# Value products from whole float32 operands, two heads in the two halves of the array

## The chip, the cores and the metric

One core of one Trainium2 chip runs the program. The metric is device time in microseconds (us) of one launch. Engines are named as in the profile: PE (TensorE matmul), PEld (its weight load), DVE (VectorE), ACT (ScalarE), POOL (GpSimd), SP (the queue that issues the DMAs).

## The reference, cut to what matters

```python
scores = q @ k.T / sqrt(64)                     # 4 batches, 8 heads, 576 positions, 64 features
keep   = scores >= max(scores, axis=-1) - tau   # the others become -1e9
attn   = exp(scores - max) over the kept / (their sum + 1e-9)
x      = (attn @ v), heads side by side         # 2304 x 512
h = x @ moe_w_in;  x = (max(h,0) + alpha*min(h,0)) @ moe_w_out     # 512 -> 2048 -> 512
h = x @ moe2_w_in; out = (h * clip(h+3,0,6)/6) @ moe2_w_out        # 512 -> 2048 -> 512
```

The four weight matrices arrive as float64, all else as float32.

## The kernel before

Everything is multiplied in float32r, the float32 form that the array takes in one pass and with fewer bits. To keep float32's accuracy an operand is split: ACT copies it to float32r (`hi`), and DVE or POOL subtracts that from the operand (`lo`, function `split`, L106). A product is then hi·hi + lo·hi + hi·lo.

Attention runs over 16 pairs of heads (4 of each batch), 9 tiles to a pair: eight tiles of 128 query rows, and one (`None` in `TILES`) with the last 64 rows of both heads. In before the four tiles of the first head come first, then `None`, then those of the second. For each tile i the loop at L608 calls, all with the scheduler's high priority:

- `prep` (L332): loads and splits q, k and v of the next pair and transposes q and k; v is loaded at tile 0 and split at tile 6 (hi and lo side by side make 128 columns, tile `vn`). `prep_t` has one product that uses only 64 rows of the array (L309).
- `do_S` (L349): scores of 576 keys, 4 products of 288 columns (8 for `None`), in one of two PSUM tiles.
- `soft_max`, `soft_thr`, `soft_exp`, `soft_keep`: maximum (DVE L372), threshold (DVE L377), exponential (ACT L382), mask and sum (DVE L389).
- `soft_den`, `soft_rc`: the sum on POOL (L395), reciprocal on DVE (L401), scaling on POOL (L403), and a second copy of the last 64 probabilities on POOL (L404).
- `do_T` (L425): four PE transposes of the float32 probabilities (L429), the hi part out of PSUM on ACT (L433), and the lo part on DVE (L438). For tiles 1, 4 and 7 of the first eight pairs PE (L435) and ACT (L436) make the lo part instead.
- `do_R` (L440): after tiles 1, 4, 6 and 8, the last 64 keys of the two or three tiles since: transposes (L448), hi on ACT (L450), lo on DVE (L451).
- `do_PV` (L453): after the same tiles, 9 float32r products against `vn`, each 256 or 320 columns wide (L465): four a pair, 36 products.
- `do_x` (L469): those products give v-hi and v-lo results in the two halves of the partitions; ACT copies one half out (L479), DVE adds (L484) into `xo`, which goes to the first FFN's input.

The two FFNs (three batches of 512 rows, then the last batch with all leftover rows) are cut into groups of 12 products of 512 columns (`h_group`, `o_group`; lines 204, 234, 240). The groups of batches 0 to 2 are queued, and from tile 39 on the loop takes from that queue after each tile, evenly to the last tile. Weights are decoded from float64 while the FFN of batch 0 runs (L127 to L144: three DVE, two ACT and one POOL instruction a chunk, 64 chunks). The order on each engine is the scheduler's. So there are four stretches: attention alone (to about 135 us of the profile), attention with FFN and decoding (to about 435), attention with FFN (to about 915), FFN alone.

Of the kernel before, what the change touches and what calls it, by code (L numbers as in the profile page):

```python
# [32 lines left out]
def kernel(  # L33
# [31 lines left out]
    PE_LO = (1, 4, 7)  # L65
    PE_LO_END = 2 * PB
    # Chunks to a sum of the output.
# [4 lines left out]
    # Columns of a batch: 128 j + p holds position 4 p + j of the first 512; the other 64  # L72
    # positions of all batches make a block of their own.
# [22 lines left out]
    nidentr = const.tile([P, P], F32R, name="nidentr")  # L96
    nc.vector.tensor_single_scalar(nidentr, ident, -1.0, op=ALU.mult)
# [65 lines left out]
    # The FFNs in their order, each with the chunks of its weights; block None is the last  # L163
    # batch together with the last positions of all.
# [90 lines left out]
    # Queries of the two heads' last positions share a tile: each head's are beside zeros.  # L255
# [5 lines left out]

    pairs = [(b, hp) for b in range(B) for hp in range(NP)]
    TILES = [(0, 0), (0, 1), (0, 2), (0, 3), None, (1, 2), (1, 3), (1, 0), (1, 1)]
# [3 lines left out]
    # A pair of heads: of the first 512 positions, 4 to a partition, a block for each of the 4;  # L267
    # the last 64 of the one head are above those of the other, in block 4 between.
    def prep_load(pi, nm):
        if pi >= len(pairs):  # L270
            return
        b, hp = pairs[pi]
        src = {"q": q, "k": k, "v": v}[nm][b, 2 * hp:2 * hp + 2]
        t = a3.tile([P, 2, NB + 1, D], F32, tag="raw", name="raw")
        nc.sync.dma_start(t[:, :, 0:NB, :].rearrange("p h j d -> p h (j d)"),
                          src[:, 0:SM].rearrange("h (p j) d -> p h (j d)", j=NB))
        if nm == "v":
            for a in range(2):
                nc.sync.dma_start(t[64 * a:64 * a + 64, :, NB, :], src[:, SM:S].rearrange("h r d -> r h d"))
        else:  # L280
            for h in range(2):
                nc.sync.dma_start(t[64 * h:64 * h + 64, 0, NB, :], src[h, SM:S])
        st.setdefault(pi, {})["raw" + nm] = t.rearrange("p h j d -> p (h j) d")

    def prep_split(pi, nm):
        raw = st[pi].pop("raw" + nm)
        n = 2 * NB + 1
        if nm == "v":
            n += 1
            t = a2.tile([P, n, 2, D], F32R, tag="vn", name="vn")  # L290
        elif pi == 0 and nm == "q":
            t = a2.tile([P, 2 * NB + 2, 2, D], F32R, tag="vn", name="natq")
# [39 lines left out]
    def prep(pi, t):  # L332
        if pi >= len(pairs):
            return
        if t == 0:
            prep_split(pi, "k")
            prep_load(pi, "v")
# [7 lines left out]
        if t == 6:  # L345
            prep_split(pi, "v")
            prep_load(pi + 1, "q")

    def do_S(i):  # L349
# [3 lines left out]
        if TILES[t] is None:  # L353
            mms = [(qr[pi % 2][:, h, :], h, a) for h in range(2) for a in range(2)]
        else:
            h, j = TILES[t]
            mms = [(s["q"][:, h * W + j * P:h * W + j * P + P], h, a) for a in range(2)]
        for half in range(2):
            for n, (w, h, a) in enumerate(mms):
                nc.tensor.matmul(ps[:, half, 0:SH], lhsT=w, rhs=s["k"][:, a, h * W + half * SH:h * W + half * SH + SH],  # L360
# [6 lines left out]
    def small(nm, bufs=2):  # L367
        return a2.tile([P, 1], F32, tag=nm, name=nm, bufs=bufs)

    def soft_max(i):  # L370
        nmx = small("nmx")
        nc.vector.tensor_reduce(out=nmx, in_=st[i, "s"][:, :, 0:SH], axis=AX.XY, op=ALU.max, negate=True)  # L372
        st[i, "nmx"] = nmx

    def soft_thr(i):
        thr = small("thr")
        nc.vector.tensor_scalar(out=thr, in0=st[i, "nmx"], scalar1=-1.0, scalar2=ntau_sb, op0=ALU.mult, op1=ALU.add)  # L377
        st[i, "thr"] = thr

    def soft_exp(i):  # L380
        e = a3.tile([P, W], F32, tag="e", name="e", bufs=5)
        nc.scalar.activation(v2(e[:, 0:S]), st[i, "s"][:, :, 0:SH], AF.Exp, bias=st.pop((i, "nmx")), scale=1.0)  # L382
        st[i, "e"] = e

    def soft_keep(i):
        e = st[i, "e"]
        sm = small("sm")
        e = e[:, 0:S]
        nc.vector.scalar_tensor_tensor(out=v2(e), in0=st.pop((i, "s"))[:, :, 0:SH], scalar=st.pop((i, "thr")), in1=v2(e),  # L389
                                       op0=ALU.is_ge, op1=ALU.mult, accum_out=sm)  # L390
        st[i, "sm"] = sm

    def soft_den(i):
        den = small("den")
        nc.gpsimd.tensor_scalar(out=den, in0=st.pop((i, "sm")), scalar1=1.0, scalar2=1e-9, op0=ALU.mult, op1=ALU.add)  # L395
        st[i, "d"] = den

    # The last 64 probabilities of a row twice.
    def soft_rc(i):
        rc = small("rc", 3)  # L400
        nc.vector.reciprocal(rc, st.pop((i, "d")))  # L401
        e = st[i, "e"]
        nc.gpsimd.tensor_scalar(out=e[:, 0:S], in0=e[:, 0:S], scalar1=rc, scalar2=0.0, op0=ALU.mult, op1=ALU.add)  # L403
        nc.gpsimd.tensor_scalar(out=e[:, S:W], in0=e[:, SM:S], scalar1=1.0, scalar2=0.0, op0=ALU.mult, op1=ALU.add)  # L404
# [3 lines left out]
    PLACE = [  # L408
        ("u", 0, None), ("u", P, (0, 0, 256)),
        ("w", 0, None), ("w", P, None), ("w", 256, (0, 0, 320)),  # L410
        ("w", 64, None), ("w", 192, (1, 64, 320)),
        ("u", 0, None), ("u", P, (1, 0, 256)),
    ]
    ptb = {}

    def pt_buf(i):
        nm = PLACE[i % NT][0]
        if i % NT in (0, 2, 7):
            ptb[nm] = a1.tile([P, 2 * NB + 1, {"u": 256, "w": 384}[nm]], F32R, tag="pt" + nm, name="pt" + nm,
                              bufs=2 if nm == "u" else 1)  # L420
        return ptb[nm]
# [3 lines left out]
    def do_T(i):  # L425
        e = st[i, "e"]
        ps = ps_t.tile([P, NB, P], F32, tag="t", name="t")
        for j in range(NB):
            nc.tensor.matmul(ps[:, j], lhsT=e[:, P * j:P * j + P], rhs=ident, is_transpose=True, start=(j == 0), stop=True,  # L429
                             skip_group_check=True)  # L430
        nm, c0, _ = PLACE[i % NT]
        pt = pt_buf(i)[:, :, c0:c0 + P]
        nc.scalar.copy(pt[:, 0:NB], ps)  # L433
        if i < PE_LO_END and i % NT in PE_LO:
            nc.tensor.matmul(ps, lhsT=nidentr, rhs=pt[:, 0:NB], start=False, stop=True, skip_group_check=True)  # L435
            nc.scalar.copy(pt[:, NB + 1:], ps)  # L436
        else:
            nc.vector.tensor_tensor(out=pt[:, NB + 1:], in0=ps, in1=f32(pt[:, 0:NB]), op=ALU.subtract)  # L438

    def do_R(i):  # L440
        nm, c0, unit = PLACE[i % NT]
        if unit is None:
            return
        m = [2, 3, 2, 2][[1, 4, 6, 8].index(i % NT)]
        ps = ps_t.tile([P, SM], F32, tag="t", name="r")[:, 0:m * P]
        for j in range(m):
            e = st.pop((i - m + 1 + j, "e"))
# [278 lines left out]
```

## Time and profile before

| | |
|---|---|
| median of 3 runs | 1220.63 us (1220.61 to 1224.99) |
| span of the profiled execution | 1219.0 us |
| PE busy | 1124.4 us, 92%, 6008 instructions |
| DVE busy | 814.9 us, 67% |
| ACT busy | 699.7 us, 57% |
| POOL busy | 770.5 us, 63% |
| DMA | 139.51 MB, 38.9% of 16 engines' span |

The median lies 1.6 us over the span of the profiled execution. The page's shares are averages over stretches that have different limits, so the stretches are read one by one. The starts of matmuls are recorded, their ends are modelled: a product's price in a row of products is the distance between starts, not its own duration.

### The profile page before, as it was taken

The numbers are of one execution on the slowest core, as the hardware profiler recorded it, in microseconds if no ns is written. First come the engines' busy times: TensorE is split into PE (matmuls) and PEld (weight loads), VectorE is DVE, ScalarE is ACT, GpSimd is POOL, SyncE is SP. The second block draws the span as 40 slices with busy tenths as digits, with TensorE's granted clock in tenths as the row PEclk, the third lists the DMA queues.
The fourth block names the chain that finished last, engine by engine and source line by source line (L and its number), as shares of the span: only waits on it lengthen the run. The fifth ranks groups of instructions, "written<-read, shape, count | busy, mean of one in ns | idle before, by whom it ended". The sixth has DMA issues, their size and how long they took to land.

```text
span 1219.0 us, 18146 instructions
## 1 busy us (share of the span) xinstructions
PE 1124.4 (92%) x6008; PEld 949.6 (78%) x6008; DVE 814.9 (67%) x1607; ACT 699.7 (57%) x1280; POOL 770.5 (63%) x917
## 2 busy tenths in 40 slices
PE   5778988987788899999999999999999999999997
PEld 4667776875576688888888888887878888888886
DVE  7999997999899967687657576777645333332221
ACT  7888865766777765555665656455644222243432
POOL 4787798889779886766556776665533443434332
PEclk9889998999989999999999999999999999999999
DMA  6732345565557453424242444232224422222211
GB/s 196 227 115 74 97 142 170 157 184 167 184 154 219 141 163 105 120 80 113 77 121 79 131 137 121 70 96 74 71 78 129 118 60 68 61 61 63 67 35 52
DMA packets 95678, 139.51 MB, mean 114 GB/s; under 512 B 21472, under 2 KB 50656, under 8 KB 95584
## 3 DMA queue, kind: packets, MB, share of 16 engines
q1 hardware_dynamic: 95584, 138.36, 38.9%
q8 instruction: 47, 0.77, 0.3%
q14 instruction: 47, 0.39, 0.1%
HBM read 103.82 MB, written 25.17 MB: 106 GB/s over the span
## 4 chain that ended last, share of the span: by engine, by line
PE 56%; DVE 4%; issue 2%; POOL 2%; ACT 1%; DMA 1%; SPq 0%; POOLq 0%; DVEq 0%; ACTq 0%
PE h L204 24%; PE o L240 11%; PE o L234 9%; PE pv L465 3%; PE s L360 3%; PE t L429 2%; PE r L234 2%; PE r L240 2%; POOL wo L108 1%; DMA st<-wo 1%; PE pt L306 1%; DVE e L389 0%; PE r L448 0%; DVE wo L108 0%; DVE g L212 0%
## 5 line engine op out<-in xcount | busy, mean ns | idle before, releaser
L204 PE MATMUL h<-x,wi 128*128 128x512 f32 (+1 forms) x1536 | 360.2, 385 | 15.9 <-DVE g L212 4.8
L204 PEld LDWEIGHTS h<-x,wi 128*128 128x128 f32 x1536 | 275.0, 190 | 74.5 <-DVE g L212 5.5
L230 POOL TENSOR_TENSOR gs<-g,gs 128x512 fp32r<-128x512 f32 (+1 forms) x160 | 194.9, 1219 | 154.6 <-ACT gs L226 149.1
L240 PE MATMUL o<-wo,gs 128*128 128x512 f32 x768 | 195.8, 396 | 5.7 <-DVE g L220 1.8
L234 PE MATMUL o<-gs,wo 128*128 128x512 f32 x768 | 195.9, 397 | 1.3 <-POOL gs L230 0.8
L240 PEld LDWEIGHTS o<-wo,gs 128*128 128x128 f32 x768 | 141.0, 188 | 36.4 <-DVE g L220 2.9
L234 PEld LDWEIGHTS o<-gs,wo 128*128 128x128 f32 x768 | 141.2, 189 | 29.6 <-POOL gs L230 1.0
L226 ACT CAST gs<-g 128x512 fp32r<-128x512 f32 (+1 forms) x160 | 92.9, 580 | 87.3 <-DVE g L212 46.2
L220 DVE SCALAR_TENSOR_TENSOR g<-m,h 128x512 f32<-128x512 f32 x80 | 50.5, 631 | 132.4 <-ACT m L218 131.9
L403 POOL TENSOR_SCALAR e<-e,rc 128x576 f32<-128x576 f32 x144 | 115.1, 804 | 20.0 <-DVE rc L401 13.9
L389 DVE SCALAR_TENSOR_TENSOR e<-s,thr,e 128x576 f32<-128x576 f32 x144 | 116.0, 813 | 9.4 <-ACT e L382 7.5
L372 DVE TENSOR_REDUCE nmx<-s 128x1 f32<-128x576 f32 x144 | 107.1, 748 | 17.0 <-PE s L360 15.5
L382 ACT ACTIVATE e<-s,nmx 128x576 f32<-128x576 f32 x144 | 106.4, 748 | 19.4 <-DVE nmx L372 11.2
L209 DVE TENSOR_SCALAR m<-h,alpha_sb 128x512 f32<-128x512 f32 x80 | 55.3, 692 | 91.9 <-PE h L204 91.9
L360 PE MATMUL s<-ka,qt 128*128 128x288 f32 x512 | 103.5, 324 | 12.7 <-DVE e L389 11.5
L107 ACT CAST wo<-st 128x512 fp32r<-128x512 f32 x99 | 59.2, 620 | 91.4 <-DMA st<-wo 81.7
L218 ACT ACTIVATE m<-h,three 128x512 f32<-128x512 f32 x80 | 51.6, 646 | 102.9 <-PE h L204 102.6
L108 POOL TENSOR_TENSOR wo<-st,wo 128x512 fp32r<-128x512 f32 x58 | 76.0, 1324 | 51.8 <-ACT wo L107 51.8
L108 POOL TENSOR_TENSOR wi<-st,wi 128x512 fp32r<-128x512 f32 x58 | 74.8, 1291 | 45.7 <-ACT wi L107 44.9
L107 ACT CAST wi<-st 128x512 fp32r<-128x512 f32 x99 | 61.2, 619 | 66.2 <-PE h L204 27.9
L429 PE MATMUL t<-ident,e 128*128 128x128 f32 x576 | 91.4, 283 | 7.9 <-ACT ptu L436 3.0
L142 POOL TENSOR_TENSOR f<-f,low 128x512 uint32<-128x512 uint32 x64 | 86.3, 1348 | 19.5 <-issue 4.0
(103 smaller groups left out, 1942.7 us busy)
## 6 DMA issues: line engine op xcount, KB each, us to landing
st<-wi SPq DMA_DIRECT2D x99, 256.0 KB, 2.6
st<-wo SPq DMA_DIRECT2D x99, 256.0 KB, 2.6
raw<-in_moe_w_in_dram SPq DMA_DIRECT2D x32, 512.0 KB, 4.1
raw<-in_moe_w_out_dram SPq DMA_DIRECT2D x32, 512.0 KB, 3.9
ka<-ka SPq DMA_DIRECT2D x30, 304.0 KB, 4.2
wi<-f SPq DMA_DIRECT2D x32, 256.0 KB, 3.1
wo<-f SPq DMA_DIRECT2D x32, 256.0 KB, 4.1
raw<-in_k_dram SPq DMA_DIRECT2D x16, 256.0 KB, 2.9
```

Source lines behind the costliest of these rows:

```text
L107: nc.scalar.copy(hi, src)
L108: lo_eng.tensor_tensor(out=lo, in0=src, in1=f32(hi), op=ALU.subtract)
L204: nc.tensor.matmul(h[:, :n], lhsT=w[:, ws, kt * P:(kt + 1) * P], rhs=x[:, xs, kt, :n], start=(i == 0), stop=(i == len(steps) - 1))
L230: nc.gpsimd.tensor_tensor(out=gs[:, 1, :n], in0=g[:, :n], in1=f32(gs[:, 0, :n]), op=ALU.subtract)
L234: nc.tensor.matmul(o[:, :n], lhsT=w[:, ws, dt * P:(dt + 1) * P], rhs=gs[:, gsel, :n], start=fresh and start and i == 0, stop=stop and i == ...
L240: nc.tensor.matmul(o[:m, :], lhsT=gs[:, gsel, tt * P:tt * P + m], rhs=w[:, ws, :], start=start and i == 0, stop=stop and i == 2)
L360: nc.tensor.matmul(ps[:, half, 0:SH], lhsT=w, rhs=s["k"][:, a, h * W + half * SH:h * W + half * SH + SH], start=(n == 0), stop=(n == len(m ...
L372: nc.vector.tensor_reduce(out=nmx, in_=st[i, "s"][:, :, 0:SH], axis=AX.XY, op=ALU.max, negate=True)
L382: nc.scalar.activation(v2(e[:, 0:S]), st[i, "s"][:, :, 0:SH], AF.Exp, bias=st.pop((i, "nmx")), scale=1.0)
L389: nc.vector.scalar_tensor_tensor(out=v2(e), in0=st.pop((i, "s"))[:, :, 0:SH], scalar=st.pop((i, "thr")), in1=v2(e), op0=ALU.is_ge, op1=ALU ...
L403: nc.gpsimd.tensor_scalar(out=e[:, 0:S], in0=e[:, 0:S], scalar1=rc, scalar2=0.0, op0=ALU.mult, op1=ALU.add)
L429: nc.tensor.matmul(ps[:, j], lhsT=e[:, P * j:P * j + P], rhs=ident, is_transpose=True, start=(j == 0), stop=True, skip_group_check=True)
```

## The change

The probabilities and the values are no longer split. `v` is loaded straight into one of two standing tiles `vs`, whose last block has each head's last 64 values beside zeros. Tiles alternate between the two heads, with `None` last. After each two tiles (and after `None`) the step `soft_norm`, `do_T`, `do_PV` runs: probabilities of both heads stand in one tile of 1152 columns, so 9 transposes serve two tiles (the last 64 keys of both heads share one), each group is copied out once by ACT as float32, and 10 float32 products follow, alternately for head 0 (output partitions 0 to 63) and head 1 (64 to 127), with 64 stationary columns and 128 moving ones (64 for `None`). One ACT copy brings the result of both heads to `xo`. The load of v moves from tile 0 to tile 2. Scores are computed as before. The core of the diff:

```diff
-    TILES = [(0, 0), (0, 1), (0, 2), (0, 3), None, (1, 2), (1, 3), (1, 0), (1, 1)]
+    TILES = [(h, j) for j in range(NB) for h in range(2)] + [None]
...
-        t = a3.tile([P, 2, NB + 1, D], F32, tag="raw", name="raw")
+        t = vs[pi % 2] if nm == "v" else a3.tile([P, 2, NB + 1, D], F32, tag="raw", name="raw")
...
         if t == 0:
             prep_split(pi, "k")
+        if t == 2:
             prep_load(pi, "v")
...
         if t == 6:
-            prep_split(pi, "v")
             prep_load(pi + 1, "q")
...
+    def soft_norm(n):
+        e, sm = st["e"]
+        den, rc = small("den", 2), small("rc", 2, 3)
+        nc.gpsimd.tensor_scalar(out=den[:, 0:n], in0=sm[:, 0:n], scalar1=1.0, scalar2=1e-9, op0=ALU.mult, op1=ALU.add)
+        nc.vector.reciprocal(rc[:, 0:n], den[:, 0:n])
+        for h in range(n):
+            eh = e[:, h * S:h * S + S]
+            nc.gpsimd.tensor_scalar(out=eh, in0=eh, scalar1=rc[:, h:h + 1], scalar2=0.0, op0=ALU.mult, op1=ALU.add)
+        if n == 1:
+            nc.gpsimd.tensor_scalar(out=e[:, S:W], in0=e[:, SM:S], scalar1=1.0, scalar2=0.0, op0=ALU.mult, op1=ALU.add)
+    def do_T(n):
+        e, _ = st["e"]
+        pt = a3.tile([P, 2 * NB + 1, P], F32, tag="p", name="p")
+        for h in range(n):
+            ps = ps_t.tile([P, NB, P], F32, tag="t", name="t")
+            for kt in range(NB):
+                c = h * W + kt * P
+                nc.tensor.transpose(ps[:, kt], e[:, c:c + P], ident)
+            nc.scalar.copy(pt[:, h * NB:h * NB + NB], ps)
+        ps = ps_t.tile([P, SM], F32, tag="t", name="r")[:, 0:P]
+        nc.tensor.transpose(ps, e[:, SM:W], ident)
+        nc.scalar.copy(pt[:, 2 * NB], ps)
+        return pt
+    def do_PV(i, n, pt):
+        pi, t = divmod(i, NT)
         b, hp = pairs[pi]
+        vn = vs[pi % 2]
+        m = P if n == 2 else SR
+        pv = ps_ho.tile([P, SM], F32, tag="ho", name="pv")[:, 0:m]
+        for kt in range(NB + 1):
+            for h in range(2):
+                blk = 2 * NB if kt == NB else kt + NB * h * (n - 1)
+                c = SR * h * (2 - n)
+                nc.tensor.matmul(pv[64 * h:64 * h + 64, :], lhsT=vn[:, h, kt, :], rhs=pt[:, blk, c:c + m],
+                                 start=(kt == 0), stop=(kt == NB), skip_group_check=True)
...
+        nc.scalar.copy(xo[:, j * P:j * P + m], pv)
```

## Rows read from the trace of the kernel before

**Rows 1.** Busy time by engine in the stretches; then share of granted clock, DMA, GB/s.

```profile
13.00:135.00 122.00, 94.76 (x593) 81.96 (x594) 114.38 (x286) 101.78 (x190) 90.64 (x153) 0.92 0.50 148
135.00:435.00 300.00, 254.87 (x1307) 208.40 (x1307) 275.19 (x501) 213.57 (x382) 258.35 (x276) 0.97 0.54 162
435.00:915.00 480.00, 471.60 (x2516) 399.79 (x2515) 324.23 (x648) 273.63 (x505) 304.70 (x380) 1.00 0.36 103
915.00:1219.00 304.00, 297.54 (x1571) 254.78 (x1569) 95.86 (x160) 102.76 (x191) 115.48 (x103) 1.00 0.25 72
```

**Rows 2.** The chain of waits from 435 to 915 us, shares by line.

```profile
by line: PE h L204 29.5%; PE o L240 14.5%; PE o L234 13.9%; PE s L360 6.6%; PE pv L465 6.6%; PE t L429 5.2%; issue 3.7%; POOL wo L108 2.6%; DMA st<-wo 1.5%; PE pt L306 1.4%; PE r L448 1.2%; DVE g L212 1.1%; DVE wo L108 1.0%; POOL nat L108 0
```

**Rows 3.** Groups by line on PE: 13 to 135, 135 to 435, 435 to 915.

```profile
L429 PE MATMUL t<-ident,e 128*128 128x128 f32 x152 | 26.7, 306 | 6.2 <-ACT ptu L436 3.0 <-POOL e L403 1.1 <-DVE ptu L438 0.7
L435 PE MATMUL t<-ptu,nidentr 128*128 128x512 f32 x8 | 3.7, 462 | 2.7 <-ACT ptu L433 2.7
...
L429 PE MATMUL t<-ident,e 128*128 128x128 f32 x152 | 23.6, 277 | 1.7 <-ACT qt L326 1.6
...
L429 PE MATMUL t<-ident,e 128*128 128x128 f32 x272 | 41.1, 274 | 0.0
L465 PE MATMUL pv<-ptw,vn 128*128 128x320 f32 x144 | 24.1, 311 | 3.3 <-DVE g L220 2.5 <-DVE acc L542 0.8
L465 PE MATMUL pv<-ptu,vn 128*128 128x256 f32 x135 | 19.3, 287 | 0.9 <-DVE g L212 0.7
```

**Rows 4.** PE in order of time: start, us, line, tile, count.

```profile
681.26 1.24 PE L465 MATMUL pv<-ptu,vn 128*128 128x256 f32 x9
...
682.47 0.37 PE L306 MATMUL pt<-identr,nat 128*128 128x128 f32 x3
682.77 0.26 PE L309 MATMUL pt<-identr,nat 64*128 64x64 f32 x1
682.96 2.35 PE L240 MATMUL o<-wo,gs 128*128 128x512 f32 x9
...
714.46 1.49 PE L465 MATMUL pv<-ptw,vn 128*128 128x320 f32 x9
...
719.34 0.60 PE L429 MATMUL t<-ident,e 128*128 128x128 f32 x4
```

**Rows 5.** Groups by line on DVE, whole span.

```profile
L438 DVE TENSOR_TENSOR ptw<-t,ptw 128x512 fp32r<-128x512 f32 x72 | 48.3, 682 | 23.3 <-ACT ptw L433 20.5 <-PE pv L465 2.7
L451 DVE TENSOR_TENSOR ptu<-r,ptu 64x256 fp32r<-64x256 f32 x32 | 13.7, 428 | 1.0
L484 DVE TENSOR_TENSOR xo<-pv,tl 64x320 f32<-64x320 f32 x32 | 15.5, 484 | 3.0 <-ACT tl L479 2.4
L401 DVE RECIPROCAL rc<-den 128x1 f32<-128x1 f32 x144 | 20.9, 152 | 2.8 <-POOL den L395 2.0
```

**Rows 6.** Groups by line on ACT, whole span.

```profile
L479 ACT COPY tl<-pv 64x320 f32<-64x320 f32 x32 | 13.4, 420 | 7.4 <-PE pv L465 6.8
L450 ACT CAST ptu<-r 128x256 fp32r<-128x256 f32 x32 | 11.9, 372 | 0.1
L107 ACT CAST vn<-raw 128x640 fp32r<-128x640 f32 x16 | 11.6, 728 | 1.1 <-DMA raw<-in_v_dram 0.8
L436 ACT CAST ptu<-t 128x512 fp32r<-128x512 f32 x16 | 9.4, 588 | 0.0
L102 ACT ACTIVATE warm<-warm 128x1 f32<-128x1 f32 x1 | 0.2, 202 | 0.0
```

**Rows 7.** Groups by line on POOL, whole span.

```profile
L404 POOL TENSOR_SCALAR e<-e 128x64 f32<-128x64 f32 x144 | 40.2, 286 | 2.3
L395 POOL TENSOR_SCALAR den<-sm 128x1 f32<-128x1 f32 x144 | 32.2, 223 | 99.1 <-DVE e L389 73.4 <-DVE rc L401 18.4
L108 POOL TENSOR_TENSOR vn<-raw,vn 128x640 fp32r<-128x640 f32 x15 | 23.5, 1569 | 11.6 <-ACT vn L107 11.6
```

**Rows 8.** DMA issues of the page: KB each, us to landing.

```profile
raw<-in_k_dram SPq DMA_DIRECT2D x16, 256.0 KB, 2.9
```

More of the change, by code (lines that the diff above doesn't have):

```diff
@@ L63 @@
     LAG = 3
-    PE_LO = (1, 4, 7)
-    PE_LO_END = 2 * PB
     OG = 4
@@ L95 @@
     nc.vector.tensor_copy(identr, ident)
-    nidentr = const.tile([P, P], F32R, name="nidentr")
-    nc.vector.tensor_single_scalar(nidentr, ident, -1.0, op=ALU.mult)
     tau_sb = const.tile([P, 1], F32, name="tau_sb")
@@ L260 @@
         qr.append(t)
+    vs = []
+    for i in range(2):
+        t = a1.tile([P, 2, NB + 1, D], F32, tag=f"v{i}", name=f"v{i}")
+        for h in range(2):
+            nc.vector.memset(t[64 - 64 * h:128 - 64 * h, h, NB, :], 0.0)
+        vs.append(t)
     pairs = [(b, hp) for b in range(B) for hp in range(NP)]
-    TILES = [(0, 0), (0, 1), (0, 2), (0, 3), None, (1, 2), (1, 3), (1, 0), (1, 1)]
+    TILES = [(h, j) for j in range(NB) for h in range(2)] + [None]
     NS = len(pairs) * NT
@@ L273, in prep_load @@
         src = {"q": q, "k": k, "v": v}[nm][b, 2 * hp:2 * hp + 2]
-        t = a3.tile([P, 2, NB + 1, D], F32, tag="raw", name="raw")
+        t = vs[pi % 2] if nm == "v" else a3.tile([P, 2, NB + 1, D], F32, tag="raw", name="raw")
         nc.sync.dma_start(t[:, :, 0:NB, :].rearrange("p h j d -> p h (j d)"),
                           src[:, 0:SM].rearrange("h (p j) d -> p h (j d)", j=NB))
+        for h in range(2):
+            nc.sync.dma_start(t[64 * h:64 * h + 64, h if nm == "v" else 0, NB, :], src[h, SM:S])
         if nm == "v":
[L278 to L282, printed above, removed]
+            return
         st.setdefault(pi, {})["raw" + nm] = t.rearrange("p h j d -> p (h j) d")
@@ L287, in prep_split @@
         n = 2 * NB + 1
[L288 to L292, printed above, removed]
+        if pi == 0 and nm == "q":
+            t = a1.tile([P, n, 2, D], F32R, tag="natq", name="natq")
         else:
@@ L353, in do_S @@
         if TILES[t] is None:
-            mms = [(qr[pi % 2][:, h, :], h, a) for h in range(2) for a in range(2)]
+            mms = [(qr[pi % 2][:, h, :], h * W, a) for h in range(2) for a in range(2)]
         else:
             h, j = TILES[t]
-            mms = [(s["q"][:, h * W + j * P:h * W + j * P + P], h, a) for a in range(2)]
+            mms = [(s["q"][:, h * W + j * P:h * W + j * P + P], h * S, a) for a in range(2)]
         for half in range(2):
-            for n, (w, h, a) in enumerate(mms):
-                nc.tensor.matmul(ps[:, half, 0:SH], lhsT=w, rhs=s["k"][:, a, h * W + half * SH:h * W + half * SH + SH],
+            for n, (w, c, a) in enumerate(mms):
+                nc.tensor.matmul(ps[:, half, 0:SH], lhsT=w, rhs=s["k"][:, a, c + half * SH:c + half * SH + SH],
                                  start=(n == 0), stop=(n == len(mms) - 1))
@@ L365, in v2 @@
         return ap.rearrange("p (a c) -> p a c", a=2)
[L367 to L404, printed above, removed]
@@ L408 @@
[L408 to L421, printed above, removed]
@@ L425, in do_T @@
[L425 to L447, printed above, removed]
-            nc.tensor.transpose(ps[:, P * j:P * j + P], e[:, SM:W], ident)
-        pt = ptb[nm][:, NB, c0 - (m - 1) * P:c0 + P]
-        nc.scalar.copy(pt, ps)
-        nc.vector.tensor_tensor(out=pt[64:P], in0=ps[64:P], in1=f32(pt[64:P]), op=ALU.subtract)
@@ L453, in do_PV, with small, soft @@
-    def do_PV(i):
+    def small(nm, n=1, bufs=2):
+        return a2.tile([P, n], F32, tag=nm, name=nm, bufs=bufs)
+    def soft(i):
+        h = 0 if TILES[i % NT] is None else TILES[i % NT][0]
+        if h == 0:
+            e = a3.tile([P, 2 * S], F32, tag="e", name="e", bufs=4)
+            st["e"] = e, small("sm", 2, 3)
+        e, sm = st["e"]
+        ps = st.pop((i, "s"))[:, :, 0:SH]
+        eh = v2(e[:, h * S:h * S + S])
+        nmx, thr = small("nmx"), small("thr")
+        nc.vector.tensor_reduce(out=nmx, in_=ps, axis=AX.XY, op=ALU.max, negate=True)
+        nc.scalar.activation(eh, ps, AF.Exp, bias=nmx, scale=1.0)
+        nc.vector.tensor_scalar(out=thr, in0=nmx, scalar1=-1.0, scalar2=ntau_sb, op0=ALU.mult, op1=ALU.add)
+        nc.vector.scalar_tensor_tensor(out=eh, in0=ps, scalar=thr, in1=eh, op0=ALU.is_ge, op1=ALU.mult, accum_out=sm[:, h:h + 1])
@@ new lines, in soft_norm @@
+    def soft_norm(n):
+        e, sm = st["e"]
+        den, rc = small("den", 2), small("rc", 2, 3)
[6 more added lines that the diff above has]
+            nc.gpsimd.tensor_scalar(out=e[:, S:W], in0=e[:, SM:S], scalar1=1.0, scalar2=0.0, op0=ALU.mult, op1=ALU.add)
@@ L454, in do_PV @@
+    def do_PV(i, n, pt):
         pi, t = divmod(i, NT)
-        nm, _, unit = PLACE[t]
-        if unit is None:
-            return
-        h, c0, n = unit
         b, hp = pairs[pi]
-        src = ptb[nm]
-        vn = st[pi]["natv"]
-        pv = ps_ho.tile([P, SM], F32, tag="ho", name="pv")
-        for kt in range(2 * NB + 1):
-            j = (NB + 1) * h + kt - (NB + 1) * (kt > NB)
-            nc.tensor.matmul(pv[:, 0:n], lhsT=vn[:, j].rearrange("p a d -> p (a d)"), rhs=src[:, kt, c0:c0 + n],
-                             start=(kt == 0), stop=(kt == 2 * NB))
@@ L467, in do_PV @@
-        st[i, "v"] = pv
-    def do_x(i):
-        pi, t = divmod(i, NT)
-        nm, _, unit = PLACE[t]
-        if unit is None:
-            return
-        h, c0, n = unit
-        b, hp = pairs[pi]
-        pv = st.pop((i, "v"))
-        hs, ls = slice(64 * h, 64 * h + 64), slice(64 - 64 * h, 128 - 64 * h)
-        tl = a1.tile([P, 320], F32, tag="tl", name="tl")[hs]
-        nc.scalar.copy(tl[:, 0:n], pv[ls, 0:n])
+        vn = vs[pi % 2]
+        m = P if n == 2 else SR
+        pv = ps_ho.tile([P, SM], F32, tag="ho", name="pv")[:, 0:m]
@@ L480, in do_x @@
+        for kt in range(NB + 1):
+            for h in range(2):
+                blk = 2 * NB if kt == NB else kt + NB * h * (n - 1)
+                c = SR * h * (2 - n)
+                nc.tensor.matmul(pv[64 * h:64 * h + 64, :], lhsT=vn[:, h, kt, :], rhs=pt[:, blk, c:c + m],
+                                 start=(kt == 0), stop=(kt == NB), skip_group_check=True)
         if "xo" not in st[pi]:
-            st[pi]["xo"] = a1.tile([P, S], F32, tag="xo", name="xo")
+            st[pi]["xo"] = a2.tile([P, S], F32, tag="xo", name="xo")
@@ L482, in do_x @@
         xo = st[pi]["xo"]
-        d0 = 0 if nm == "u" else 256
-        nc.vector.tensor_tensor(out=xo[hs, d0:d0 + n], in0=pv[hs, 0:n], in1=tl[:, 0:n], op=ALU.add)
-        if t == NT - 1:
+        j = t // 2
+        nc.scalar.copy(xo[:, j * P:j * P + m], pv)
+        if n == 1:
             if b == 0:
@@ L602 @@
         prep_t(0, nm, r)
-    prep_split(0, "v")
     prep_load(1, "k")
@@ L612 @@
             do_S(i)
-            soft_max(i)
-            soft_thr(i)
-            soft_exp(i)
-            soft_keep(i)
-        with tc.high_priority(offset=50):
-            soft_den(i)
-            soft_rc(i)
-            do_T(i)
-            do_R(i)
-            do_PV(i)
-            do_x(i)
+            soft(i)
+        if t % 2 == 1 or t == NT - 1:
+            with tc.high_priority(offset=50):
+                n = 1 + t % 2
+                soft_norm(n)
+                do_PV(i, n, do_T(n))
         if i % PB == PB - 1:
```

## Prediction

> **What bounds the kernel now.** I read the busy time of each engine by stretch first, then the chain of waits of the longest stretch, then the groups by line, and last PE's instructions in order of time, because the change swaps one kind of product for another and only the distance between starts prices those.
>
> The table by stretch [rows 1] shows four different limits. From 13 to 135 us (attention alone) DVE is busy 114.4 of 122 us, 94%; PE has 94.8, ACT 101.8, POOL 90.6. From 135 to 435 (attention, FFN, decoding) DVE has 275.2 of 300, 92%, and PE 254.9 and POOL 258.4 are close behind. From 435 to 915 PE has 471.6 of 480, 98.2%, at granted clock 1.00, and nobody else is over 325. From 915 on there is no attention, so nothing changes there. The chain of 435 to 915 [rows 2] agrees: products of the FFNs, scores, value products and transposes fill most of it, and DVE's lo parts (L438) are not among its shares. So the change is worth what it takes from DVE in the first two stretches, as far as PE, ACT and POOL let the gain through, and it costs in the third whatever it adds to PE. Counted in transposes of four to a tile [rows 3], the stretches hold 38, 38 and 68 tiles, that is 4.2, 4.2 and 7.55 of the 16 pairs.
>
> **What it takes from DVE, POOL and ACT, for one pair.** DVE: nine lo parts L438 go (six in the first eight pairs) at 0.68 us, four of the last keys L451 at 0.43, four sums L484 at about 0.45 (the wide ones 0.48), and four of nine reciprocals L401 at 0.15 [rows 5]. That is 6 x 0.68 + 1.7 + 1.8 + 0.6 = 8.2 us in the first eight pairs, 10.2 after. POOL: eight of nine second copies L404 at 0.29, four of nine L395 at 0.22, the lo part of v at 1.57 [rows 7]: 2.3 + 0.9 + 1.6 = 4.8 us. ACT: four L450 at 0.37 and four L479 at about 0.4 go, the hi part of v at 0.73, and in the first eight pairs three L436 at 0.59 [rows 6]. New on ACT are five copies of 128 columns of transposes and five of products. No row has that width: 0.37 for 256 columns is the upper bound and 0.20 for one column the lower [rows 6]; I take 0.28, between them, 2.8 us in all. Net: 1.0 us less a pair, 2.8 less in the first eight.
>
> **What it takes from PE.** The 36 value products start 0.147 us apart at 320 columns ((1.49 - 0.31)/8) and 0.119 at 256 ((1.24 - 0.29)/8) [rows 3, 4]: 18 of each, 4.8 us. Of 45 float32 transposes four go. They start (0.60 - 0.27)/3 = 0.109 us apart [rows 3, 4], so 0.4 us. The three L435 in each of the first eight pairs have 512 columns, like L240 with (2.35 - 0.4)/8 = 0.24 [rows 3, 4]: 0.7 us. Score products stay: 40 a pair, whatever the order of tiles.
>
> **What it gives to PE.** 40 float32 products of 128 columns and ten of 64: 45 of 128, if columns set the price. No row shows a float32 product that is not a transpose; this is the large unknown. The nearest row has the type and the moving width: the transpose at 0.109. The same width in float32r (L306) starts about (0.37 - 0.25)/2 = 0.06 apart [rows 4], so whole float32 costs almost twice. In a transpose the moving side is an identity and each value passes alone. A product of two whole numbers needs the other half of the stationary side as well, so I double the transpose: 0.218. It lies among three or four float32r products of 128 columns (0.18 to 0.24), which is what the kernel's own split arithmetic would need. Lower end: 0.109 (as a transpose, or 0.218 with the two heads fully at once). Upper end: if what separates 0.109 from 0.06 is a weight load that nothing covers, and the product pays it twice more, 0.218 + 2 x 0.048 = 0.314. I take 0.218 one after another, because in every row of the trace products start one after another, and no row shows two at once.
>
> A rule of the Trainium skill weighs on the first factor: "FP8 and Floating Point Precision", TensorE Precision Notes, gives four passes to a true float32 product. At the full clock, 2.4 GHz, that would be an estimated 4 x 128 columns, 0.213 us, and the sum below; by the transpose's row alone the sum would be that of the first rival. The trace so far shows two of the four at most.
>
> Each group of value products also changes the array's shape, to 64 columns and back. The nearest row is the product on 64 rows, L309: three L306 and the change take 682.47 to 682.77, 0.30 us, of which two distances are 0.12; 0.18 is left where 0.06 is usual. The way back takes 682.77 to 682.96, 0.19 [rows 4]. I take 0.12 each way; five groups a pair make 1.2 us (0 if halves of columns change nothing).
>
> Sum for PE: 45 x 0.218 + 1.2 - 4.8 - 0.4 = +5.8 us a pair, +5.1 in the first eight.
>
> **What is moved.** The load of v (three DMAs as before) goes from tile 0 to tile 2 on SP, past two tiles' weight fetches, and now waits until the last value products of the pair before have read its buffer. Those are issued three tiles earlier: 480/68 = 7.1 us a tile in the third stretch, 122/38 = 3.2 in the first. Landing takes some 3 us, by k's row [rows 8], and the first reader comes eight tiles later, so the cover is some 25 us even in the first stretch. If the buffer is late, SP holds k's next load and weight fetches behind it. I price that at nothing; without the cover, at most a tile for each of the four first pairs, 13 us. Alternating heads, and two tiles to a normalization, lengthen one tile's way but leave four tiles of 1152 columns in flight, more than before: nothing.
>
> **The sum**, against the profiled execution (1219.0; the median lies 1.6 above). I let each stretch end at the share that its limit reaches today.
> - 13 to 135: DVE 114.4 - 4.2 x 8.2 = 80; ACT 90; POOL 70; PE 94.8 + 4.2 x 5.1 = 116. PE becomes the limit: 116/0.982 = 118, so -4. The DVE gain is nearly all lost.
> - 135 to 435: DVE 241, POOL 238, PE 254.9 + 21.4 = 276; 276/0.982 = 281, so -19.
> - 435 to 915: PE 471.6 + 7.55 x 5.8 = 515; 515/0.982 = 525, so +45. What is late next is again PE; the relief of DVE has nowhere to go.
>
> -4 - 19 + 45 = +22: 1241 in that execution, **1243 us** as a median. With waits and the shape changes between 0 and 0.2 us this spreads over 1222 to 1262.
>
> **Rival 1, faster: the two halves of columns work at once.** Head 0 and head 1 alternate and use different output partitions; if a product of one head streams while the other's does, the price is 0.109 each. Against it: the rows show strict succession; for it: none of them had two products in different columns. PE then gains 45 x 0.109 + 1.2 - 5.2 = +0.9 a pair (+0.2 early). First stretch: 95.5/0.94 = 102, -20; second: 256/0.92 = 279, -21; third: +7. Together -35, **1186 us**. It decides below about 0.175 us a product, where the line between the two sums crosses today's time. The Trainium skill, "TensorEngine Tiling (Array Packing)", Key Properties, states this rule: different tiles of the array can load and multiply in parallel. No row here shows it.
>
> **Rival 2, half of that.** Alternating products overlap only in part, because the halves of one float32 product must follow each other: 0.16 each, midway, **1214 us**.
>
> **Rival 3, weight loads exposed.** At 0.314, PE pays 4.3 us more a pair than in my sum; every stretch is PE's by then: 15.95 x 4.3/0.98 = +70, **1313 us**. For it: the excess of the float32 transposes over float32r; against it: 64 columns are half a load.
>
> **How the numbers follow.** Forecast 0.50, rival 1 0.22, rival 2 0.12, rival 3 0.16. About 0.5% is what a measurement of this kernel can tell from no change: 1214.5 to 1226.7. Faster: rival 1, half of rival 2 and the low edge of the forecast, 0.30. Same: the rest of rival 2 and some of the forecast, 0.13. Slower: 0.57. The likeliest's own range is 1222 to 1262; to hold eight in ten it must reach to half of rival 1 (1187) and to nearly half of rival 3 (1305).
>
> **What would show it.** The starts of the new products: 0.2 us and more apart, or two within 0.11. PE's share in 13 to 135 rising to 95% and DVE's falling to about 65%. Busy DVE near 668, POOL near 694, ACT near 670 over the span: these hold under every rival, as the work is counted; if they don't, parts are not as I read them. The third stretch growing to some 525 us. I am wrong if the heads overlap, if the new groups leave gaps at their ends much over 0.12 us, or if PE in the first stretch waits for its chain instead of filling.

## The result, and the profile after

The changed kernel takes 1210.93 us (median; 1206.91 to 1211.51) against 1221.29 of the kernel before on the same chips: a ratio of 0.9903, 95% interval 0.9881 to 0.9925. It is 10 us faster. The forecast was 1243, slower; the time lies in the stated range, on the other side of the kernel before. The profiled execution spans 1205.1 us, 13.9 less than that of before; it is the shortest of its four, 4 us under their median, so its marks show somewhat more than the median gained.

Busy time by engine in the stretches of [rows 1] (columns: stretch and its length, then PE, PEld, DVE, ACT, POOL busy with their counts, granted clock, DMA share, GB/s), in the changed kernel:

```profile
13.00:135.00 122.00, 109.18 (x915) 88.05 (x915) 96.63 (x234) 96.52 (x200) 80.95 (x109) 0.96 0.55 157
135.00:435.00 300.00, 262.14 (x1569) 213.03 (x1568) 251.45 (x429) 209.31 (x388) 250.17 (x225) 0.97 0.57 172
435.00:915.00 480.00, 472.77 (x2932) 389.70 (x2931) 233.99 (x464) 250.67 (x489) 260.47 (x269) 1.00 0.33 96
```

Against [rows 1], DVE fell from 94% to 79% of the first stretch and PE rose from 78% to 89%, at a granted clock of 0.96 instead of 0.92. From 435 on PE is as full as before, at the same clock. The stretches themselves have moved, though. Three lines mark their ends: the last decoding step on POOL, the first product of an FFN, the last value product. The view is one line's instructions (count, duration in ns, first and last start in us); after, then before:

```profile
L137 POOL TENSOR_TENSOR f<-f,low x64: 1259/1294/1482, 25.4 to 410.8; 128x512 uint32<-128x512 uint32 x64
L199 PE MATMUL h<-x,wi x1536: 274/389/628, 129.4 to 1059.0; 128*128 128x512 f32 x176, 128*128 128x256 f32 x16
L425 PE MATMUL pv<-p,v x1600: 222/273/476, 22.6 to 910.6; 128*64 128x128 f32 x142, 128*64 128x64 f32 x36
```

```profile
L142 POOL TENSOR_TENSOR f<-f,low x64: 1267/1298/1770, 24.1 to 432.2; 128x512 uint32<-128x512 uint32 x64
L204 PE MATMUL h<-x,wi x1536: 275/390/797, 137.5 to 1072.5; 128*128 128x512 f32 x176, 128*128 128x256 f32 x16
L465 PE MATMUL pv<-ptu,vn x288: 274/282/583, 23.8 to 924.2; 128*128 128x256 f32 x144
```

| stretch | before | after | difference |
|---|---|---|---|
| start to the first FFN product | 137.5 | 129.4 | -8 |
| from there to the last decoding step | 294.7 | 281.4 | -13 |
| from there to the last value product | 492.0 | 499.8 | +8 |
| from there to the end | 294.8 | 294.5 | 0 |

The first row shows less than attention gained. The fourth pair's result becomes the first FFN's input (its hi part, on ACT) at 120.7 us instead of 137.2, in order of time (start, us), after and before:

```profile
120.07 0.62 ACT L102 CAST x<-xo 128x512 fp32r<-128x512 f32 x1
```

```profile
136.57 0.62 ACT L107 CAST x<-xo 128x512 fp32r<-128x512 f32 x1
```

The first FFN product follows 8.7 us later instead of 0.3; in between PE works on the fifth pair. Why it comes so late was not tested.

And this is what the forecast turned on, PE in order of time (start, us, line, tile, count):

```profile
710.15 1.31 PE L425 MATMUL pv<-p,v 128*64 128x128 f32 x20 [1.19 <-DVE g L207]
...
729.01 0.80 PE L425 MATMUL pv<-p,v 128*64 128x64 f32 x20
```

Ten products are twenty records, two to a product (1600 for 800 above). Twenty records take 1.31 us, of which the last one's own duration is 0.27. Within the row the starts come in pairs 6 ns apart, one of each head (e1 shows that), and each pair 0.109 after the last (0.16 after the first): 0.109 us a product, half of what the forecast paid. In the second row, of 64 moving columns, the pairs start 0.058 apart.

### The profile page after: what moved, and what is told of

It is laid out like the page before. It is cut to its first block, busy times and chain, and to the rows that moved or that the text cites. A ratio compares the mean times of both kernels' runs of the same rounds, so it can differ in the third digit from the quotient of the medians.

```text
span 1205.1 us, 19458 instructions
## 1 busy us (share of the span) xinstructions
PE 1133.9 (94%) x6944; PEld 939.0 (78%) x6944; DVE 678.6 (56%) x1297; ACT 662.8 (55%) x1272; POOL 703.9 (58%) x710
## 4 chain that ended last, share of the span: by engine, by line
PE 60%; DVE 3%; issue 1%; POOL 1%; DMA 1%; ACT 1%; DVEq 0%; POOLq 0%; ACTq 0%
PE h L199 25%; PE o L235 12%; PE o L229 11%; PE s L361 3%; PE pv L425 3%; PE t L407 2%; PE r L229 2%; PE r L235 2%; DMA st<-wo 1%; DVE m L204 1%; DVE g L207 1%; PE pt L306 1%; POOL wo L103 0%; DVE g L215 0%; PE r L410 0%
## 5 line engine op out<-in xcount | busy, mean ns | idle before, releaser
L199 PE MATMUL h<-x,wi 128*128 128x512 f32 (+1 forms) x1536 | 356.6, 381 | 2.9 <-DVE g L207 1.0
L425 PE MATMUL pv<-p,v 128*64 128x128 f32 (+1 forms) x1600 | 109.7, 273 | 9.3 <-DVE g L215 6.7
L425 PEld LDWEIGHTS pv<-p,v 128*64 128x64 f32 x1600 | 84.8, 139 | 31.8 <-issue 15.1
```

Source lines behind the costliest of these rows:

```text
L199: nc.tensor.matmul(h[:, :n], lhsT=w[:, ws, kt * P:(kt + 1) * P], rhs=x[:, xs, kt, :n], start=(i == 0), stop=(i == len(steps) - 1))
L425: nc.tensor.matmul(pv[64 * h:64 * h + 64, :], lhsT=vn[:, h, kt, :], rhs=pt[:, blk, c:c + m], start=(kt == 0), stop=(kt == NB), skip_group_ ...
```

## The experiments

Each ran beside the kernel before, whose median was 1221 to 1222 in every set. The edits are to the changed kernel. "Last decoding step" and "parts" (unbroken rows of value products; 80 groups would be 80 parts at the least, and the changed kernel has 108) are counted in each trace, that is in one execution; executions of one kernel lie up to 6.4 us apart (e4, e5), so a few us between the marks of two traces may be chance.

| run | median us | ratio to before | 95% interval | last decoding step | parts |
|---|---|---|---|---|---|
| the changed kernel | 1210.93 | 0.9903 | 0.9881 to 0.9925 | 410.8 | 108 |
| e1 heads in turn | 1242.89 | 1.0181 | 1.0158 to 1.0203 | 420.3 | 107 |
| e2 full width | 1260.19 | 1.0317 | 1.0296 to 1.0337 | 424.9 | 113 |
| e3 lo parts back | 1215.10 | 0.9950 | 0.9932 to 0.9968 | 417.4 | 116 |
| e4 POOL work back | 1214.28 | 0.9946 | 0.9928 to 0.9963 | 418.4 | 106 |
| e5 DVE in the chain | 1224.22 | 1.0013 | 0.9997 to 1.0030 | 427.3 | 107 |
| e6 four tiles | 1205.99 | 0.9871 | 0.9847 to 0.9895 | 409.4 | 63 |
| e7 no clamp | 1182.35 | 0.9678 | 0.9657 to 0.9699 | 385.5 | 109 |
| e8 no scaling | 1195.88 | 0.9789 | 0.9757 to 0.9821 | 400.7 | 110 |
| e9 all back | 1223.60 | 1.0012 | 0.9997 to 1.0026 | 430.7 | 104 |
| e10 products later | 1204.52 | 0.9859 | 0.9835 to 0.9883 | 403.0 | 99 |
| e11 v at tile 0 | 1214.79 | 0.9945 | 0.9923 to 0.9967 | 419.5 | 110 |
| e12 four tiles, later | 1190.51 | 0.9747 | 0.9727 to 0.9768 | 400.9 | 57 |

### e1: the two heads in turn

```diff
-        for kt in range(NB + 1):
-            for h in range(2):
+        for h in range(2):
+            for kt in range(NB + 1):
```

> The changed kernel, but each group of value products does all five of head 0 first and then all five of head 1; the work and the shapes are the same. Theory (the two heads' products stream at once in the two halves of the columns, 0.109 us each, and the order makes that possible): in turn they start 0.218 us apart, PE pays 45 x 0.109 = 4.9 us more a pair; PE is the limit after the first pair and again from the end of decoding on, so about 16 + 6 + 38 = 60 us more than the changed kernel, some 1270 us. Rival (a float32 product costs 0.109 by itself, set by its weight load or its stream, and overlap has no part in it): the time of the changed kernel, 1211 us.

Measured: 1242.89 us, 32 more than the changed kernel, with not an instruction added. PE in order of time:

```profile
734.36 2.02 PE L425 MATMUL pv<-p,v 128*64 128x128 f32 x20 [0.72 <-DVE g L207]
```

The same twenty records take 2.02 us instead of 1.31, so the rival is out: order alone decides. Only 32 of the 60 us that I expected came, for two reasons. A group is not twice as long. Its starts are 0.109 apart for the first seven records (0.16 after the first), then two rows interleave, 0.05 apart, from 735.07 to 735.45, then 0.109 again: head 1 begins while about three of head 0's records are still to come. And the stretches ahead of 411 us took up some of the rest: decoding ends 9.5 us later, where I expected 22. From there to the last value product it is 524.4 us instead of 499.8, 25 more, where I expected 38.

### e2: one shape for all

```diff
-        t = a1.tile([P, 2, NB + 1, D], F32, tag=f"v{i}", name=f"v{i}")
+        t = a1.tile([P, 2, NB + 1, 2 * D], F32, tag=f"v{i}", name=f"v{i}")
...
-                nc.tensor.matmul(pv[64 * h:64 * h + 64, :], lhsT=vn[:, h, kt, :], rhs=pt[:, blk, c:c + m],
-                                 start=(kt == 0), stop=(kt == NB), skip_group_check=True)
+                nc.tensor.matmul(pv, lhsT=vn[:, h, kt, :], rhs=pt[:, blk, c:c + m],
+                                 start=(kt == 0 and h == 0), stop=(kt == NB and h == 1))
```

The load of v is cut as well, to fit the wider tile: head by head, in rows of 64 columns.

> The changed kernel with a stationary operand of 128 columns: each head's 64 values beside 64 columns of zeros, both heads summed into the same result. No shape change is left and no overlap is possible. Theory (a change of the array's shape costs about 0.1 us each way, on top of the serial price): no gap of 0.2 us at the ends of a group; 0.218 us a product; faster than the version with heads in turn by 16 pairs x some 7 groups or parts of groups x 0.2 = 20 us at most, 10 to 15 where PE is the limit, so about 1255 us. Rival (the gaps at the ends are the drain of float32 products, not of the shape): as the version in turn, 1270 us, with the same gaps.

Measured: 1260.19 us, slower than e1 by 17; both expected times missed. PE in order of time:

```profile
730.26 2.39 PE L429 MATMUL pv<-p,v 128*128 128x128 f32 x20
732.41 0.94 PE L199 MATMUL h<-x,wi 128*128 128x512 f32 x3
```

The gaps did go, as the theory said: the next product starts 2.15 us after the group's first, 19 steps of 0.112 and one of 0.03. In the changed kernel an unbroken group holds PE 1.24 us for ten pairs of 0.109 (the median of 47 groups; the one at 710.15 above holds it 1.38). But each record is 0.112 apart, 0.224 a product, and so are those of 64 moving columns, which take 0.058 a record in the changed kernel. So with 128 stationary columns of whole float32 the moving columns don't set the price; that the weight load does is likely, and no run shows it apart. What the ends of a part cost can be read from the steps of the changed kernel: its first record starts 0.20 us after a transpose, the second pair 0.16 after the first, and what follows 0.20 after the last record, where the usual step is 0.109 each time. That is 0.24 us together, what I had taken from L309. In e2 a transpose is 0.11 from the group on either side.

### e3 and e4: the removed work put back, unused

```diff
+            lo = a1.tile([P, NB, P], F32, tag="lo", name="lo")
+            nc.vector.tensor_tensor(out=lo, in0=ps, in1=pt[:, h * NB:h * NB + NB], op=ALU.subtract)
```

> The changed kernel with the nine subtractions of 128 x 512 a pair put back on DVE; their result is not used. Theory (DVE's relief is what shortened the two stretches before the end of decoding, 8 to 14 us of the first and 13 of the second): most of it goes, decoding ends at some 425 to 430 us instead of 411, about 1222 us. Rival (PE and the chain of decoding set those stretches and DVE has room for 98 us more): 1211 to 1214 us.

```diff
+        for h in range(n):
+            two = a2.tile([P, SR], F32, tag="two", name="two")
+            nc.gpsimd.tensor_scalar(out=two, in0=e[:, h * S:h * S + SR], scalar1=1.0, scalar2=0.0, op0=ALU.mult, op1=ALU.add)
...
+            vlo = a1.tile([P, 2, NB + 1, D], F32, tag="vlo", name="vlo")
+            nc.gpsimd.tensor_tensor(out=vlo, in0=vs[pi % 2], in1=vs[pi % 2], op=ALU.subtract)
```

> The changed kernel with POOL's removed work put back, result unused: a 64-column copy for each tile and the subtraction of 128 x 640 a pair, 4 us a pair. Theory (POOL was close to the limit while weights are decoded, but DVE was the one): within 3 us of the changed kernel. Rival (POOL's relief, 4.2 pairs x 4 = 17 us, made the gain of that stretch): 1220 to 1225 us.

Measured: 1215.10 and 1214.28 us, 4.2 and 3.4 over the changed kernel. The theory of e3 fell; e4 lies 0.4 us beyond what its theory allowed. DVE's busy time rose by 76 us (754.2 against 678.6) and POOL's by 54 (757.5 against 703.9). Neither load explains the gain alone. How little these differences carry is shown by e11: it only moves a load, and it is as far off. The scheduler plans the whole order anew for each edit (the same 80 groups fall into 106 to 116 parts in e1 to e5), and 4 us may be no more than that.

### e5: DVE back in the chain

```diff
-            nc.scalar.copy(pt[:, h * NB:h * NB + NB], ps)
+            hi = a2.tile([P, NB, P], F32, tag="hi", name="hi")
+            nc.scalar.copy(hi, ps)
+            nc.vector.tensor_tensor(out=pt[:, h * NB:h * NB + NB], in0=ps, in1=hi, op=ALU.max)
```

> The changed kernel, but the transposed probabilities reach the value products by way of DVE, as in the kernel before: ACT copies them out of PSUM, and DVE takes the larger of that copy and the PSUM tile (the same numbers) into the operand. DVE's load is that of the run with the lo parts put back (1215.1 us, 4 us over the changed kernel); new is that the products wait for DVE. Theory (the change gained by taking DVE out of the way from transpose to product, more than by its load): 1220 us or more. Rival (only load counts, and it counts little): 1215 us.

Measured: 1224.22 us, 13 over the changed kernel and 9 over e3, whose DVE is just as busy (754.2 and 757.0). All of the change's gain is gone. The new line among DVE's groups, and the two marks:

```profile
L410 DVE TENSOR_TENSOR p<-t,hi 128x512 f32<-128x512 f32 x144 | 95.8, 680 | 9.7 <-ACT hi L409 5.4 <-PE pv L427 4.2
```

```profile
L137 POOL TENSOR_TENSOR f<-f,low x64: 1264/1294/1492, 26.9 to 427.3; 128x512 uint32<-128x512 uint32 x64
L199 PE MATMUL h<-x,wi x1536: 274/389/776, 144.0 to 1075.7; 128*128 128x512 f32 x176, 128*128 128x256 f32 x16
```

The first FFN product starts at 144.0 (129.4 in the changed kernel, 137.9 in e3), the last decoding step at 427.3 (410.8, 417.4), and what follows takes 499.9 as in the changed kernel. So DVE's place between transpose and product counts more than its load, and it counts in the two stretches ahead of the end of decoding alone, 6.1 and 3.9 us against e3. How it counts is only in part seen. The value products hardly wait for the new step (0.4 us in the trace). Those that do are the next transposes, L412 and L407: 6.2 us, 3.3 (PEld) and 3.9, against 0.3, 0.5 and 2.0 in e3. They don't read the operand; they share the PSUM tiles that the step reads.

### e6, e10, e12: fewer parts, later products

e6 gathers four tiles in `pt` (256 moving columns) and multiplies after tiles 3, 7 and `None`. e10 issues the products of two tiles after the transposes of the next two. e12 does both; this is its diff, cut.

```diff
-        m = P if n == 2 else SR
+        m = 2 * P if n == 2 else SR
...
                 soft_norm(n)
-                do_PV(i, n, do_T(n))
+                pt = do_T(n, t // 2 % 2)
+                if "late" in st:
+                    do_PV(*st.pop("late"))
+                if n == 1:
+                    do_PV(i, n, pt)
+                elif t // 2 % 2 == 1:
+                    st["late"] = i, n, pt
```

> The changed kernel with a group of value products after every four tiles instead of two: half as many products of twice the columns (256), so three groups a pair instead of five, and half the weight loads. Theory (each group or part of a group costs PE about 0.19 us for the change of the array's shape and back, 108 parts in the changed kernel): some 40 parts fewer, 8 us of PE, 6 of it where PE is the limit: 1205 us. Rival (longer groups wait for more tiles and hold PSUM and the array longer, which gives it back): 1211 us or more.

> The changed kernel with the value products of two tiles issued after the transposes of the next two (those of a pair's last tile at once). The work is the same. Theory (28 of 80 groups are cut in parts because their last operands are still being copied, and each part costs 0.19 us): nearer to 80 parts, 5 us of PE, 1207 us. Rival (the scheduler's order already places them as late as it pays, and later products keep PSUM and buffers longer): 1211 us or more.

> Both e6 (groups of four tiles) and e10 (products after the next tiles' transposes). Theory: the parts of groups fall to the least there can be, 48; 3 us under e6, 1203 us. Rival (no more than e6 or e10 alone, as PE's wait is then for something else): 1206 us or more.

Measured: 1205.99, 1204.52 and 1190.51 us. e6 has the time that was expected, but not where: it has 45 parts fewer, and yet from the last decoding step to the last value product it takes 501.9 us, no less than the changed kernel's 499.8. (Its profiled execution is the longest of its four, 1207.88, so where the 5 us of its median lie can't be read.) In e10, 2.5 us under its theory, the parts fell to 99 only, and the gain is ahead: the first FFN product starts at 120.9 instead of 129.4, though the fourth pair's result is there only 2.2 us earlier (118.5, not 120.7). From the end of decoding on it loses 4 us (504.1). e12 lies far under both expectations, and its parts are 57, not 48. Together the two edits give more than the sum, 20 us under the changed kernel and 31 under the kernel before, with the last two stretches at 492.8 and 294.9. The marks of e12, and PE in order of time at the end of a pair:

```profile
L137 POOL TENSOR_TENSOR f<-f,low x64: 1263/1299/1613, 26.6 to 400.9; 128x512 uint32<-128x512 uint32 x64
L199 PE MATMUL h<-x,wi x1536: 274/389/796, 124.3 to 1042.4; 128*128 128x512 f32 x176, 128*128 128x256 f32 x16
```

```profile
712.39 2.96 PE L427 MATMUL pv<-p,v 128*64 128x256 f32 x40
715.28 3.02 PE L229 MATMUL o<-gs,wo 128*128 128x512 f32 x12
```

These 40 records are a group of four tiles, whose pairs start 0.216 apart, and the group of `None` after it, 0.058 apart: 2.89 us until the next product, with one pair of ends for what the changed kernel does in three groups. That fewer parts and an earlier operand are worth little alone and much together is measured; why is only argued: fewer parts help where PE doesn't wait at their starts anyway, and products issued later don't.

### e7 and e8: what sets the stretch of decoding

```diff
-        nc.vector.tensor_scalar(out=f32(f), in0=f32(f), scalar1=F64_HI, scalar2=F64_LO, op0=ALU.min, op1=ALU.max)
```

> The changed kernel without the clamp of decoded weights, which leaves 54 us of DVE out, nearly all of it while weights are decoded (so weights under float32's range are not treated right). Theory (in that stretch no engine is at its limit, DVE is busy 86%, and the ordered chain of decoding sets it): the time moves by under 6 us, 1205 or more. Rival (DVE still sets the stretch in bursts): most of the 54 us that fall there, divided by what the next engines leave, about 20 us: 1190.

```diff
-        for h in range(n):
-            eh = e[:, h * S:h * S + S]
-            nc.gpsimd.tensor_scalar(out=eh, in0=eh, scalar1=rc[:, h:h + 1], scalar2=0.0, op0=ALU.mult, op1=ALU.add)
```

> The changed kernel without the scaling of the probabilities by their reciprocal sum (left out, so the attention is not normalized), which takes 117 us from POOL, some 31 of it while weights are decoded, and one step of 0.8 us from each tile's chain. Theory (POOL is no more the limit there than DVE): under 6 us, 1205 or more. Rival (POOL sets that stretch): 15 us or more, 1195.

Measured: 1182.35 and 1195.88 us, -29 and -15. My theory fell in both; e8 came to its rival's 1195, and e7 below its rival's 1190. In e7 the stretch from the first FFN product to the last decoding step shrinks from 281.4 to 254.6 us, and the one after it stays (500.3). The stretch in the changed kernel and in e7:

```profile
129.00:411.00 282.00, 244.39 (x1452) 197.73 (x1451) 241.82 (x411) 195.71 (x362) 236.54 (x216) 0.96 0.57 173
```

```profile
132.00:385.00 253.00, 233.04 (x1441) 191.67 (x1440) 197.17 (x355) 193.07 (x359) 230.22 (x213) 0.99 0.61 191
```

In the changed kernel PE, DVE and POOL stand at 84 to 87% there, so I had said that none of them sets it. But 45 us of DVE less in that stretch are 27 us less of time, 0.6 for each. The clamp is both load on DVE and a step of each chunk's way through the engines; e7 doesn't tell the two apart. For the way speaks that load beside it hardly shows: e3 puts 35 lo parts, 23.7 us, into that stretch, which takes 279.4 us. This is no clean contrast, as DVE's busy time there rises by 8 us only (249.4), in part because the decoding steps take less each (L135 0.75 us instead of 0.83). In e8, of 11 us between the two profiled executions, 7 are gone before the first FFN product (122.7 instead of 129.4) and 3 in the stretch of decoding (278.0); the scaling, too, is both load on POOL and a step of each tile's way.

### e9: all back

e5 and e4 together.

> The changed kernel with DVE in the chain (as in e5) and POOL's removed work back (as in e4), so that of the change only PE's part, some ACT copies and the shorter normalization are left. Theory (the gain is the sum of DVE's place in the chain and load, 13 us, and POOL's load, 3 us, less what PE pays more after the end of decoding, 8 us): all of it given back, and PE's extra cost shows: 1211 + 13 + 3 = 1227 us, some 6 over the kernel before. Rival (with DVE in the chain POOL's load no longer counts): as e5, 1224 us; or other parts of the change (tile order, larger tiles) carry gain of their own: under 1221.

Measured: 1223.60 us, as e5. The theory's 1227 fell, and the first rival holds: with DVE in the chain, POOL's load adds nothing. The kernel before stands at 1221.55 in that set, so what is left of the change after that, PE's dearer products against ACT's and DVE's smaller savings, lies between 0.4 us of gain and 3 of loss. In the trace decoding ends at 430.7 us, against 410.8 in the changed kernel and 432.2 before: what the change gained up to there goes when the removed work comes back, most of it (427.3) with e5 alone.

### e11: the load of v at tile 0

```diff
-        if t == 2:
             prep_load(pi, "v")
```

> The changed kernel with the load of v back at tile 0 of the pair before instead of tile 2, so it is queued one tile after the last products that read its buffer instead of three. Theory (the place of this load costs nothing): 1209 to 1213 us. Rival (a load that waits for the products holds the weight fetches behind it): 1216 us or more.

Measured: 1214.79 us, 3.9 over the changed kernel, between the two expectations. The step that I priced at nothing is worth 4 us or the new plan of the order is; this run can't tell.

## Why the prediction went wrong, point by point

**The failed step** is the price of a value product: "I take 0.218 one after another, because in every row of the trace products start one after another, and no row shows two at once." The doubling of the transpose was right: a product is two records of 0.109. "One after another" was wrong: the two heads' records start 6 ns apart. e1, which takes that overlap away for most of each group and leaves all else, measures 1242.89 where the forecast for strict succession was 1243. That it meets the forecast so closely is luck: two misses cancel. Its end of decoding is 12 us earlier than before, where the forecast had 23, and its stretch after that 32 us longer (524.4 against 492.0), where the forecast had 45. The term decides the sign: at 0.109 the same sum is that of rival 1, 57 us lower. It doesn't explain the whole time, as the rest of the sum then misses by 25 us the other way. The reason that I gave is where the mistake lies: no row could have shown two at once, because no two products of the kernel before lie in different columns. The absence of a case was read as a rule. The Trainium skill's sentence on parallel tiles in "TensorEngine Tiling (Array Packing)", Key Properties, is what the trace then showed, with starts 6 ns apart. The four passes of the Trainium skill ("FP8 and Floating Point Precision", TensorE Precision Notes) agree too, as 0.218 us for the two records of 128 columns.

**Rival 1, which had the mechanism, gave 1186**, 25 us too low: -20, -21 and +7 in the first three stretches, -8, -13 and +8 measured. So 21 are missing from the two early ones; the other 4 are the distance of the profiled execution from its median. The third is right: 16 pairs x 100 records cost what the rival said, and the ends of parts 0.24 us together, though there are 6.75 parts a pair and not five. In the first stretch I let the whole of it end at its busiest engine's share. The first pair is as long as before (why, no run tested): the first maxima on DVE of the second to the fifth pair start at 42.1, 68.5, 90.8 and 111.7 us, against 41.5, 74.7, 100.8 and 125.0. So the second pair takes 26 us instead of 33, and the next two 22 and 21 instead of 26 and 24, better than assumed, and there PE is indeed the limit, as the forecast had it for its own reasons:

```profile
71.00:113.00 42.00, 41.13 (x396) 34.12 (x396) 31.75 (x82) 34.71 (x77) 25.61 (x40) 1.00 0.35 94
```

Another part of the gap is the late first FFN product: the fourth pair's result is 16 us earlier, near the rival's 20. In the second stretch I took 34 us off DVE's busy time and let the next engine end it. But what shortens that stretch is a step less on the way of decoding (e7), of which DVE's lo parts were no part (e3, with the doubt named there).

**What DVE's relief was worth** I counted by load, 8 to 10 us a pair. e5 against e3 shows that the load was the smaller thing: 4 us, perhaps no more than a new plan of the order moves, while DVE's place between transpose and product is worth 9 more. The text had no line for a step that leaves a chain. How the place acts is open; the waits of e5 point at the PSUM tiles.

**What was right.** The work, counted: DVE 668 forecast and 678.6 measured, POOL 694 and 703.9, ACT 670 and 662.8. The small ACT copies, bounded by 0.20 and 0.37 and taken as 0.28:

```profile
L411 ACT COPY p<-r 128x128 f32<-128x128 f32 x80 | 22.2, 277 | 5.8 <-PE r L410 5.7
L431 ACT COPY xo<-pv 128x128 f32<-128x128 f32 x64 | 17.1, 267 | 12.6 <-PE pv L425 12.3
```

The change of the array's shape, 0.12 each way from L309 [rows 4]: 0.24 for both in the steps. That PE is the limit from 435 us on and whatever is added there is paid in full: +8 us, and more clearly e2, where nothing overlaps. There 50 products of 0.224 are 11.2 us a pair, where I had 45 x 0.218 + 1.2 = 11.0, and the stretch after decoding is 536.8 us, 45 more than before, as forecast. The place of v's load is not settled (e11).

**Open:** what the decoding chain waits for at each step, what holds the first FFN product, how DVE's place acts, why e6 and e10 add up to more than their sum, and whether 4 us of e3, e4 and e11 are theirs or the scheduler's.

## What to carry to other kernels

Where two products write different halves of the array's columns, order them alternately and price them as one: the same instructions in turn cost 32 us here. Where a trace cannot contain a case, its absence says nothing and must not count against it; find a row that could have shown it, or say that there is none. And ask of a step that is removed from an engine what came after it: 0.68 us of DVE put back between transpose and product cost 13 us here, and the same load put back beside that way 4.

## What the runs showed of the hardware

- A float32 product of 128 moving columns on 64 stationary ones is two records of 0.109 us; of 64 columns, two of 0.058; of 256 (e12), two of 0.216. Two such rows in the two halves of the columns run at once, 6 ns apart.
- With 128 stationary columns of float32 a record takes 0.112 us whether 64 or 128 columns move (e2). That the weight load sets it is likely and not shown.
- In e1 the second head's first record starts some three records before the first head's last. If the starts were in program order, the seventh and eighth record of one head would have started 6 ns apart, which no two of one head do elsewhere.
- The ends of a part, from 128 columns to 64 and back, cost PE 0.24 us together over the usual steps, and nothing of it is left where the shape stays (e2).
